# A gated mix of one-token attention and a dense layer: where w2's first half is loaded and multiplied

## The chip, the cores and the metric

The kernel runs on one core of a Trainium2 chip. The metric is the device time of one execution in microseconds (us), the median of several runs. Besides the times there is one profiled execution with its trace: TensorE's products (PE) and weight loads (PEld), VectorE (DVE), ScalarE (ACT), GpSimd (POOL), SyncE (SP, which issues nearly all loads), and the DMA engines. "Span" is the time from the first to the last instruction of that execution.

## The reference

One token with D = 576 values. The attention half has 32 query heads over 16 key/value heads, a window of the last 4096 keys and a head size of 128; the other half is a dense layer with 4608 hidden values and a GELU. A sigmoid gate mixes the two.

```python
g = sigmoid((x * gate_w).sum(-1, keepdims=True))
# A: attention on the last W = 4096 keys
q = x @ wq                                    # 32 heads of 128
k, v = k_cache[:, :, Sk - W:], v_cache[:, :, Sk - W:]
p = softmax(einsum("bhqd,bhkd->bhqk", q, k) * Dh ** -0.5)
a = einsum("bhqk,bhkd->bhqd", p, v).reshape(1, 1, 4096) @ wo
# B: the dense layer
b = gelu(x @ w1 + b1) @ w2 + b2
out = g * a + (1 - g) * b                     # [1, 1, 576]
```

All inputs are bfloat16. Everything is read once: w1 and w2 (5184 KB each), wq and wo (4608 KB each), and 16 MB each of keys and values, 53.6 MB in all.

## The kernel before

**Stages.** The kernel multiplies x by w1, builds the GELU's result `gt` (already scaled by 1 - g, 36 columns of 128 values), multiplies x by wq, and then goes through the keys in four groups of four key/value heads (`k_t`, 4096 KB each). VectorE transposes each half of a group (L550), TensorE makes the scores, ACT the exponentials. The values come in four tiles as well (`v_t`, 4096 KB each); `value_products(g)` (L660) multiplies tile g by the transposed probabilities, 32 products of 512 columns, in four column groups of the array side by side. `own_sums(g)` reduces the result on VectorE and `outputs(g)` (L694) brings it into `o_ps`. With all four, VectorE scales by the gate and the sums of the exponentials (`om`, `om_t`), five small products rearrange the heads into `ov_ps`, and two copies make `ov` (VectorE) and `ov_tail` (ACT).

**The end.** The result row is accumulated in `y_ps`. `y_add(vec, row)` (L384) adds one column of 128 values times one row tile of a weight: two products, 272 and 304 columns, in two column groups of the array, which run side by side. wo takes 4 such rows from a small part loaded apart (`wo_tail`, multiplied by `ov_tail`) and 31 from `wo_t` (multiplied by `ov`); w2 takes 36 (multiplied by `gt`), 18 in each half. Two copies and one store of 1.1 KB end the program.

**Order of the loads.** SyncE issues the loads in program order, each as soon as its buffer is free, and one queue serves them. The large buffers are four, tagged A to D. The keys take C, D, B, A, then values 0 and 1 take C and D (free when the keys in them are transposed), w2 takes B, values 2 A, values 3 C again (after value products 0), wo D (after value products 1). So the order behind the keys is: v0, v1, w2's first half (L646), v2, the two small loads of wo, v3, wo (L752), and w2's second half in four pieces of 10, 5, 2 and 1 rows (L757). A DMA tells of its landing by a semaphore; a small set of them is used in turn, so that an issue can also wait for an earlier load that has the same one.

**Order on TensorE.** The order is written out: `queue("pe", ...)` (L526) places each step behind the one queued before it. Around the change it is: value products 3; rows 0 to 5 of w2; outputs(3); rows 6 and 7; the five small products of `ov_ps`; rows 8 to 17; then the list `late` (L807): the four rows of `wo_tail`, one unused product, the 31 rows of `wo_t`, the 18 rows of w2's second half.

**The unused product.** `None` in `late` stands for a product of 512 f32 columns (the memory of the probabilities `p_t`, read as f32) by `ones`, written to `spare`, half of a PSUM tile that nobody reads (L815).

## Time and profile before

| what | value |
|---|---|
| median of 3 runs | 131.41 us (131.40 to 131.53) |
| the profiled execution | 131.67 us, its span 130.3 us |
| mean granted TensorE clock | 0.817 of full speed |
| DMA | 53.67 MB, mean 412 GB/s over the span |
| busy: PE, DVE, ACT, POOL | 79.3, 61.0, 11.5, 10.0 us |
| products of w2 rows (72) and wo_t rows (62) | 6.3 and 4.2 us busy |
| v2, v3 from issue to landing | 21.9 and 23.7 us |

Busy time of PE counts overlapping products once, and ends of products are modelled. The name of w1 and of w2 is shortened to `w_t` in the profile (digits are left out), `p_t` and `pt` are the probabilities, `s_ps` is any of the large PSUM tiles, and the tail of wo appears as `zeros`, the tile it lies in. A DMA's time "to landing" runs from its issue to its last semaphore update, and holds the time for which it waits behind earlier loads in the queue.

### The profile page before, as it was taken

How to read it: one execution, taken by the hardware profiler on the slowest of the kernel's cores; microseconds unless marked ns; L12 is line 12 of the kernel's file. 1: busy time of each engine (PE TensorE's matmuls, PEld its weight loads, DVE VectorE, ACT ScalarE, POOL GpSimd, SP SyncE). 2: the span in 40 equal slices, each digit the busy share in tenths (PEclk: the TensorE clock that was granted, in tenths of full speed). 3: DMA queues.
4: the chain of work that ended last, by engine and by line, in shares of the span. 5: the costliest groups of instructions: out<-in, count | busy, mean ns of one | idle time of the engine just before them, and what ended most of it. 6: DMA issues, size and time to landing. Idle time of an engine off the chain costs nothing.

```text
span 130.3 us, 1142 instructions
## 1 busy us (share of the span) xinstructions
PE 79.3 (61%) x538; PEld 26.2 (20%) x412; DVE 61.0 (47%) x50; ACT 11.5 (9%) x27; POOL 10.0 (8%) x32
## 2 busy tenths in 40 slices
PE   0003899297106996859949946995300840789794
PEld 0003012110100221211211210132200320245572
DVE  0030006215199769999999995145900050051001
ACT  3032100300300000030003003003000000000001
POOL 7009800100000000000000000000010000000000
PEclk9999999658755799985999995599655577579999
DMA  7999999899899999989989989999989999898970
GB/s 249 404 437 432 475 419 475 364 473 473 362 453 473 408 402 473 433 382 473 443 372 473 453 362 473 391 458 443 443 372 477 444 392 475 384 493 356 407 294 15
DMA packets 2503, 53.67 MB, mean 412 GB/s; under 512 B 286, under 2 KB 418, under 8 KB 708
## 3 DMA queue, kind: packets, MB, share of 16 engines
q1 hardware_dynamic: 2490, 53.61, 96.3%
q8 instruction: 3, 0.05, 0.2%
q10 hardware_dynamic: 10, 0.01, 0.0%
HBM read 53.62 MB, written 0.00 MB: 412 GB/s over the span
## 4 chain that ended last, share of the span: by engine, by line
DMA 60%; DVE 21%; PE 13%; issue 5%; ACT 0%; DVEq 0%
DMA k_t<-in_A_k_cache_dram 31%; DMA wo_t<-in_A_wo_dram 25%; DVE kt L550 15%; PE y_ps L386 5%; PE s_ps L572 5%; DMA rows<-in_A_x_dram 5%; DVE m L588 3%; DVE pt L621 2%; PE s_ps L662 1%; PE acc L662 1%; DVE mr L591 1%; ACT out_row L828 0%; PE mt_ps L597 0%; DVE negm L605 0%; DVEq L550 0%
## 5 line engine op out<-in xcount | busy, mean ns | idle before, releaser
L572 PE MATMUL s_ps<-kt,qz_flat 128*128 128x512 bf16 x128 | 35.3, 436 | 15.1 <-DVE kt L550 8.3
L550 DVE STREAM_TRANSPOSE kt<-k_t 128x4096 f32<-128x4096 f32 x8 | 35.3, 4432 | 4.8 <-DMA k_t<-in_A_k_cache_dram 4.8
L662 PE MATMUL s_ps<-v_t,pt 128*32 128x512 bf16 x96 | 9.1, 547 | 12.0 <-DMA v_t<-in_A_v_cache_dram 12.0
L572 PEld LDWEIGHTS <-qz_flat 128*128 128x128 bf16 x64 | 7.2, 112 | 40.6 <-issue 40.4
L676 DVE TENSOR_TENSOR own<-s_ps,is 128x512 f32<-128x512 f32 x3 | 2.1, 688 | 18.9 <-PE s_ps L662 18.9
L609 ACT ACTIVATE p_t<-s_ps,negm 128x1024 bf16<-128x1024 f32 x4 | 4.5, 1114 | 50.0 <-DVE negm L605 50.0
L662 PEld LDWEIGHTS <-pt 128*32 128x32 bf16 x128 | 3.7, 117 | 17.5 <-DMA v_t<-in_A_v_cache_dram 12.2
L342 PE MATMUL xs_ps<-ident,rows 1*128 1x1 bf16 x9 | 0.6, 189 | 10.8 <-POOL ident masks.py:199 10.8
L407 PE MATMUL s_ps<-w_t,x 128*32 128x512 bf16 x36 | 6.0, 611 | 1.6 <-DVE x L350 1.6
L588 DVE TENSOR_REDUCE m<-s_ps 128x1 f32<-128x1024 f32 x4 | 4.8, 1195 | 3.9 <-PE s_ps L572 3.9
L386 PE MATMUL y_ps<-w_t,gt 128*1 128x272 bf16 (+1 forms) x72 | 6.3, 304 | 0.0
L407 PE MATMUL s_ps<-wq_t,x 128*32 128x512 bf16 x36 | 4.9, 619 | 2.2 <-DMA wq_t<-in_A_wq_dram 2.2
L621 DVE STREAM_TRANSPOSE pt<-p_t 128x1024 bf16<-128x1024 bf16 x4 | 4.9, 1224 | 2.7 <-ACT p_t L609 2.7
L432 DVE STREAM_TRANSPOSE turned<-s_ps 128x1024 f32<-128x1024 f32 x2 | 2.5, 1249 | 7.3 <-PE s_ps L407 7.2
L829 DVE CAST out_row<-y_ps 1x272 bf16<-1x272 f32 x1 | 0.4, 429 | 10.2 <-PE y_ps L386 10.2
L713 POOL TENSOR_TENSOR ls<-is,sums 128x32 f32<-128x32 f32 x1 | 0.2, 240 | 63.9 <-ACT p_t L609 63.9
L697 PE MATMUL mt_ps<-is,summed 128*128 128x8 f32 x8 | 2.0, 319 | 4.6 <-DVE summed L686 4.6
L386 PE MATMUL y_ps<-wo_t,ov 128*1 128x272 bf16 (+1 forms) x62 | 4.2, 286 | 0.8 <-DMA wo_t<-in_A_wo_dram 0.8
L356 DVE CUSTOM_DVE_ANT_0 rows<-rows 1x576 bf16<-1x576 bf16 x1 | 0.7, 746 | 8.3 <-DMA rows<-in_gate_w_dram 8.3
L386 PEld LDWEIGHTS <-gt 128*1 128x1 bf16 x72 | 4.0, 89 | 1.9 <-issue 0.7
L686 DVE TENSOR_REDUCE summed<-own 128x128 f32<-128x512 f32 x4 | 4.2, 1044 | 0.1
L487 DVE STREAM_TRANSPOSE q_turned<-s_ps 128x1024 f32<-128x1024 f32 x2 | 2.4, 1228 | 3.8 <-PE s_ps L407 3.8
(83 smaller groups left out, 51.9 us busy)
## 6 DMA issues: line engine op xcount, KB each, us to landing
k_t<-in_A_k_cache_dram SPq DMA_DIRECT2D x4, 4096.0 KB, 33.9
v_t<-in_A_v_cache_dram SPq DMA_DIRECT2D x4, 4096.0 KB, 22.8
wq_t<-in_A_wq_dram SPq DMA_DIRECT2D x1, 4608.0 KB, 25.0
wo_t<-in_A_wo_dram SPq DMA_DIRECT2D x1, 4464.0 KB
w_t<-in_B_w_dram SPq DMA_DIRECT2D x1, 2880.0 KB, 14.4
w_t<-in_B_w_dram SPq DMA_DIRECT2D x1, 2592.0 KB, 23.6
w_t<-in_B_w_dram SPq DMA_DIRECT2D x1, 2304.0 KB, 8.3
w_t<-in_B_w_dram SPq DMA_DIRECT2D x1, 1440.0 KB
```

The costliest lines, as they stand in the source:

```text
L386: last = nc.tensor.matmul(y_out[s], lhsT=vec, rhs=row[:, DH:D] if s else row[:, 0:DH], start=start, stop=stop, skip_group_check=True,)
L407: nc.tensor.matmul(last[n][32 * g : 32 * g + 32], lhsT=vec, rhs=part(n), start=start and g0 == 0, stop=g0 + 4 + g >= len(pieces), skip_gro ...
L432: nc.vector.transpose(out=turned[:, c0 : c0 + n], in_=src[:].rearrange("p (q l j) -> p q j l", q=q, l=32),)
L487: nc.vector.transpose(out=q_turned[:, 1024 * c : 1024 * c + 1024], in_=q_s[c][:].rearrange("p (h l b) -> p h b l", l=32, b=2),)
L550: lambda: nc.vector.transpose(out=kt[g, f][:].bitcast(FP32), in_=keys.rearrange("p c d -> p (c d)").bitcast(FP32),),
L572: last = nc.tensor.matmul(s_ps[g][:, u * 512 : (u + 1) * 512].rearrange("p (c k) -> p c k", k=32), lhsT=qz(g, j, 2 * f + half), rhs=kv[:, ...
L588: queue("dve", lambda: nc.vector.reduce_max(out=m1[:], in_=s_ps[g][:], axis=AX.X))
L609: nc.scalar.activation(out=p_t[:].rearrange("p c k -> p (c k)"), in_=s_ps[g][:], func=ACT.Exp, bias=negm[:, 0:1], scale=SCALE, accum_out=s ...
L621: lambda: nc.vector.transpose(out=pt[:, g, :, :].rearrange("p c q -> p (c q)"), in_=p_t[:].rearrange("p c k -> p (c k)"),),
L662: last = nc.tensor.matmul(acc[g][32 * (c % 4) : 32 * (c % 4) + 32, :], lhsT=pt[:, g, c, :], rhs=v_t[g][:, c:NCK:32, :], start=(c < 4), sto ...
L676: lambda: nc.vector.tensor_tensor(out=own[:], in0=acc[g].rearrange("p (c d) -> p c d", c=4), in1=same_c.rearrange("p (c o) -> p c o", o=1) ...
L686: lambda: nc.vector.tensor_reduce(out=summed[g][:], in_=own[:].rearrange("p c d -> p d c"), axis=AX.X, op=ALU.add,),
```

## The change

The load of w2's first half moves from between v1 and v2 to behind wo. Its 18 rows, until now in three places among the value tile's steps, move into `late`, behind the 31 rows of `wo_t`. The one unused product between `wo_tail`'s rows and `wo_t`'s becomes four; one more of 512 columns goes behind `wo_t`'s rows, and one of 256 columns between the two halves of w2.

```diff
     v_t = [load("v_t", "CD"[g], A_v_cache, g) for g in range(2)]
-    nc.sync.dma_start(out=w2_t[:, 0:NJ, :], in_=w2_src[:, 0])
     v_t.append(load("v_t", "A", A_v_cache, 2))
...
+    nc.sync.dma_start(out=w2_t[:, 0:NJ, :], in_=w2_src[:, 0])
     for j0, j1 in ((0, 10), (10, 15), (15, 17), (17, 18)):
         nc.sync.dma_start(out=w2_t[:, NJ + j0 : NJ + j1, :], in_=w2_src[:, 1, j0:j1, :])
 
-    def w2_rows(f0, f1):
-        for f in range(f0, f1):
-            queue("pe", lambda: y_add(gt[:, f : f + 1], w2_t[:, f, :]))
-
-    w2_rows(0, 6)
     outputs(3)
...
-    w2_rows(6, 8)
     ov_ps = ps_m.tile([P, RO + 4], FP32, name="ov_ps", tag="m")
...
-    w2_rows(8, NJ)
     late = [(ov_tail, j, wo_tail[:, j, :]) for j in range(4)]
-    late.append(None)
+    late += [512] * 4
     late += [(ov, r, wo_t[:, r, :]) for r in range(RO)]
+    late += [512]
+    late += [(gt, f, w2_t[:, f, :]) for f in range(NJ)]
+    late += [256]
     late += [(gt, f, w2_t[:, f, :]) for f in range(NJ, NF)]
     for n, item in enumerate(late):
-        if item is None:
+        if isinstance(item, int):
             queue(
                 "pe",
                 lambda: nc.tensor.matmul(
-                    spare,
+                    spare[:, 0:item],
                     lhsT=ones[:],
-                    rhs=p_t[:].rearrange("p c k -> p (c k)").bitcast(FP32),
+                    rhs=p_t[:].rearrange("p c k -> p (c k)").bitcast(FP32)[:, 0:item],
                     start=True,
                     stop=True,
                 ),
```

## The prediction

> **What bounds the kernel now.** I read the profiled execution as a whole first, then its end. It took 131.67 us: a span of 130.3 us and 1.37 us around it. The median of the three timed runs is 131.41 us, so 0.26 us is taken off at the end of the sum. The page's 40 slices, in tenths:

> ```profile
> PEclk9999999658755799985999995599655577579999
> DMA  7999999899899999989989989999989999898970
> ```

> The DMA engines are full until the last few slices (53.67 MB at a mean of 412 GB/s), and TensorE's clock is at half speed for long stretches. The chain of waits (start us, us, what) ends so:

> ```profile
> 89.91 32.07 DMA wo_t<-in_A_wo_dram
> 121.97 0.04 issue
> 122.01 6.60 PE y_ps L386 x90
> 128.61 0.02 issue
> 128.63 0.40 ACT out_row L828
> ```

> As if TensorE's last 6.60 us set the end. The DMA view (KB each, us from issue to landing) and the view of the w2 and w1 loads (ns min/median/max, first and last start in us) correct that:

> ```profile
> w_t<-in_B_w_dram SPq DMA_DIRECT2D x1, 2592.0 KB, 23.6
> w_t<-in_B_w_dram SPq DMA_DIRECT2D x1, 288.0 KB, 36.2
> w_t<-in_B_w_dram SPq DMA_DIRECT2D x1, 144.0 KB, 27.0
> L757 SPq DMA_DIRECT2D w_t<-in_B_w_dram x4: 328/388/583, 90.5 to 101.3; - x4
> ```

> The last piece of w2 (144 KB, issued at 101.3) lands at 101.3 + 27.0 = 128.3, and in the same view the products with w2 start from 114.8 to 128.3. The end is a tie: the load queue drains just as TensorE reaches the last row. From there 0.3 us of products, 0.40 us of copy and the store follow in any version. So earlier work on TensorE gains nothing, and later work costs in full.

> TensorE's timeline between the last value tile and the end (start us, us, engine, line, tiles, count, idle before):

> ```profile
> 111.46 3.60 PE L662 MATMUL s_ps<-v_t,pt 128*32 128x512 bf16 x32 [4.29 <-DMA v_t<-in_A_v_cache_dram]
> 114.84 1.46 PE L386 MATMUL y_ps<-w_t,gt 128*1 128x272 bf16 x12
> 116.94 0.39 PE L697 MATMUL mt_ps<-is,summed 128*128 128x8 f32 x2 [0.63 <-DVE summed L686]
> 118.10 1.46 PE L386 MATMUL y_ps<-w_t,gt 128*1 128x272 bf16 x20
> 119.48 0.68 PE L386 MATMUL y_ps<-zeros,ov_tail 48*1 48x272 bf16 x8
> 120.09 1.12 PE L815 MATMUL s_ps<-p_t,ones 128*128 128x512 f32 x2
> 122.01 3.78 PE L386 MATMUL y_ps<-wo_t,ov 128*1 128x272 bf16 x59 [0.80 <-DMA wo_t<-in_A_wo_dram]
> ```

> The rows of w2's first half fill the gaps between 114.84 and 119.5. Twelve such products take 1.46 us at 114.84, twenty take 1.46 us at 118.10: the clock doubled in between. Half-microsecond windows (window, us, busy per engine, then granted clock, DMA share, GB/s) show when it changes:

> ```profile
> 85.00:85.50 0.50, 0.50 (x4) 0.04 (x1) 0.00 (x0) 0.00 (x0) 0.00 (x0) 0.82 0.68 290
> 105.50:106.00 0.50, 0.00 (x0) 0.00 (x0) 0.47 (x2) 0.00 (x0) 0.00 (x0) 0.84 0.46 197
> 109.00:109.50 0.50, 0.00 (x0) 0.00 (x0) 0.00 (x0) 0.00 (x0) 0.00 (x0) 0.57 0.78 334
> 115.50:116.00 0.50, 0.50 (x9) 0.43 (x4) 0.47 (x2) 0.00 (x0) 0.00 (x0) 0.60 0.99 429
> ```

> **The change, part by part.**

> *The moved load.* w2's first half is issued at 68.11 and lands 23.6 us later, at 91.7. Behind it v2 lands at 101.3, v3 at 111.4 and wo at 122.0 (the chain's row). v3 to wo is 4464 KB in 10.55 us, v2 to v3 4240 KB (v3 and the two small wo loads) in 10.1 us: 420 KB/us, so 2592 KB are 6.2 us. Without it ahead of them v2 lands at 95.1, v3 at 105.3, wo at 115.8; w2's first half takes wo's old place at 122.0, and the pieces behind it keep theirs, up to 128.3. The same bytes go through the same queue, so the last landing is unchanged: 0. The issue itself (0.33 us of SyncE) moves to about 90.5, ahead of the four pieces, which need not start before 122. SyncE's own waits show 9.2 us before the fourth piece until v2 lands; with one load fewer ahead in the turn of semaphores it is the third piece that waits for v2 (95.1), and the fourth for a small wo load: both before 102, and harmless. Cover in the queue: v2, issued at 79.37, had w2's half in front of it until 91.7, 12.3 us; now only v1 until 85.5, 6.1 us. The program's first load (2304 KB) took 8.3 us to land, of which 5.5 are transfer at 420 KB/us, so starting costs at most 2.8 us: 3.3 us are to spare, price 0. v3 (87.74) has v2 until 95.1, more than enough.

> *The removed rows.* 36 products leave the stretch 114.84 to 119.5 (1.46 + 0.42 + 1.46 us with the four at 117.26). TensorE stood idle 0.80 us at the end of it, waiting for wo: their place was free, so removing them frees nothing on the path. Added behind wo they do cost. wo's rows, from 122.01 to the last start at 125.89, are 30 steps of 0.129 us, so 18 rows (36 products, two side by side) are 2.3 us.

> *The unused products.* One of 512 columns holds TensorE from 120.09 to 121.15, its own weight loads included: 1.06 us at full clock. Four in a row are at most 4.2 us; at least 3.4 us, if their weight loads are hidden (a 512-column round of the value products at full clock is (1.91 - 0.38) / 7 = 0.22 us, and an f32 product of this row is two matmuls, each lasting one round longer, 592 against 379 ns, so four rounds each). I take 3.6, since the second weight load already runs under the first product. One of 256: half of 0.85 plus 0.2 of changeover, 0.6.

> *The sum.* Value tile 3 starts at 105.3. From its start (111.46) to ov_tail's copy (118.43 + 0.16) is 7.13 us, a chain through VectorE that the removed rows did not hold up: tail rows start at 112.4. At full clock: tail rows 0.6 (119.48 to 120.09), four products 3.6, wo's 31 rows 4.0, one product 1.06, w2's first 18 rows 2.3, the half product 0.6, the last 18 rows 2.3, end of the last product 0.2: 14.7 us, to 127.1. wo (115.8) and w2's first half (122.0) are there by the time they are wanted (116.6 and 121.7), or nearly. The landing bound is 128.3 + 0.3 = 128.6, as before. At full clock the change would be hidden, by 1.5 us.

> It will not be at full clock. Before, dense work from 111.46 on had raised it by 115.90, and nothing later let it fall. Now value tile 3 ends at 108.8 and TensorE has some 1 us of work until 112.4: a stretch like that of 105.66 to 109.07, after which the clock fell. The tail rows start at half speed, and stay there for T us, which costs T/2. T is 3.0 at break-even. Shortest: about 2.4, if a step falls just as they start (a stretch with 2.4 us of work, 78.35 to 81.77, did not raise it, one with about 2.6 of value products, 102.25 to 105.66, did). Longest: the 5.8 seen. The three seen give 2.2, 2.2 and 2.9 us of loss, 0.7 to 1.4 us beyond the cover; the short end gives none. I take T = 4.1, between the two ends: 127.1 + 2.05 = 129.15 against 128.60, **0.55 us later**. 131.67 + 0.55 - 0.26 = **131.95 us**. With T = 5.8 it is 132.8; with the products' upper price 0.6 more.

> [...]

> **Rivals.** *Hidden after all*: T at or below 3.4, or a shorter sum, and the queue sets the end: 131.4 us. For it: 1.5 us of cover, and a step at 109.07, as in this trace, lets the clock fall right at 112.5 and rise at 115.90, T = 3.5, a loss of 0.25 only. Against: two of the three rows. Chance 0.34. *Faster*: the queue ends unevenly; the DMA share falls to 0.60 at 125.5 and about 0.43 in the microsecond after 126, so if the new order evened out the engines the last landing could come up to 1.5 us sooner. TensorE allows 127.1 + 1.2 = 128.3, a gain of 0.3: 131.1 us, only where T is below 3. Against: each engine moves the same bytes in either order. 0.04. *The f32 products or one-column rows don't count as busy*: then half speed lasts through all four (8.4 us) and a stretch more, T about 11, 135.4 us. Against: the clock held at full speed from 115.90 to the end on little else. 0.03. *The queue runs dry* at v2, because starting costs more than 6.1 us in a full queue: each microsecond costs one, 132.4 us for one. 0.03.

> **How the numbers follow.** The forecast, late by 0.2 to 1.4 us, has 0.56. About 0.2% (0.26 us) is what a measurement of this kernel can tell from no change. Slower: 0.56 + 0.03 + 0.03 = 0.62; same: 0.34; faster: 0.04. The range reaches from just under the hidden case, 131.3, to the longest T, 132.9; the forecast's own is 131.6 to 132.9.

> **What would show it.** The last piece of w2 lands at 128.3 in both traces; value tile 3 starts at 105.3; wo's rows start at 117.5 to 119 with no wait for wo; the clock is 0.5 when the tail rows start and rises 2.4 to 5.8 us later; the last rows run without waiting for w2 and end 0.2 to 1.4 us after 128.6. I am wrong if TensorE waits for w2's last piece (hidden), if that piece lands elsewhere than at 128.3, or if the clock is already full at 112.4.

## The result, and the profile after

The changed kernel takes 132.77 us (median of 6 runs, 132.19 to 132.96) where the old one takes 131.41 (131.17 to 131.56): a ratio of 1.0096, 95% interval 1.0075 to 1.0118, or 1.36 us later. The profiled execution took 132.96 us with a span of 131.4. On another chip, beside the experiments below, it was 132.61 against 131.56 us. Medians here and below are of all runs, while ratios leave out a run that is more than 1.5% above the fastest of its kernel, as two runs of experiment 6 and two of experiment 9 are.

The end of the chain of waits of the changed kernel (start us, us, what):

```profile
86.67 18.08 DMA v_t<-in_A_v_cache_dram
104.75 0.04 issue
104.79 3.46 PE s_ps L661 x32
...
111.58 0.16 ACT ov_tail L798
111.75 0.04 issue
111.79 1.17 PE y_ps L386 x8
112.97 6.22 PE s_ps L811 x8
119.19 4.10 PE y_ps L386 x59
123.28 1.06 PE s_ps L811 x2
124.34 2.42 PE y_ps L386 x35
126.76 0.63 PE s_ps L811 x2
127.39 2.43 PE y_ps L386 x35
129.84 0.40 ACT out_row L824
```

No DMA stands between v3's landing and the end: from 111.79 on TensorE never waits. The old chain ended with a load of wo and products that just kept up with the last pieces of w2; this one ends with TensorE alone, at 129.84 in place of 128.61, 1.23 us later. Four unused products (L811 x8) take 6.22 us, and the rows of wo, which landed at 115.3, wait for them until 119.1. The copy of `ov_tail` is followed by eight tail products in 1.17 us, where they took 0.68 before.

Windows of the changed kernel (window, us, busy per engine, granted clock, DMA share, GB/s), cut at the clock's steps, which lie whole multiples of 3.41 us apart here as before (rises at 97.67, 107.91 and 118.15, falls at 101.08 and 111.32):

```profile
107.91:111.32 3.41, 1.15 (x15) 0.50 (x4) 2.14 (x4) 0.00 (x0) 0.00 (x0) 1.00 1.07 461
111.32:114.73 3.41, 2.94 (x10) 1.26 (x11) 0.19 (x1) 0.16 (x1) 0.00 (x0) 0.50 0.93 401
114.73:118.15 3.42, 3.42 (x5) 1.35 (x4) 0.00 (x0) 0.00 (x0) 0.00 (x0) 0.50 1.00 423
```

Full speed until 111.32, since the step ahead of it (104.49 to 107.91) held 3.12 us of value tile 3; then half speed for two whole steps, to 118.15. The first of these had TensorE busy for 2.94 of 3.41 us and still did not raise the clock. The tail rows started at 111.79, so half speed lasted T = 118.15 - 111.79 = 6.36 us of the 18 that follow.

The loads moved as worked out: v2 in use at 95.07, v3 at 104.79, wo landed at 115.3. The 288 KB piece, issued at 95.05, landed 32.4 us later, at 127.4; the last piece followed at 127.8, where the old order had 127.9 and 128.3.

### The profile page after: what moved, and what is told of

It is laid out like the page before. It is cut to its first block, busy times and chain, and to the rows that moved or that the text cites. A ratio compares the mean times of both kernels' runs of the same rounds, so it can differ in the third digit from the quotient of the medians.

```text
span 131.4 us, 1161 instructions
## 1 busy us (share of the span) xinstructions
PE 81.8 (62%) x548; PEld 28.8 (22%) x422; DVE 61.0 (46%) x50; ACT 11.5 (9%) x27; POOL 10.0 (8%) x32
## 4 chain that ended last, share of the span: by engine, by line
DMA 49%; PE 22%; DVE 22%; issue 5%; ACT 0%; DVEq 0%
DMA k_t<-in_A_k_cache_dram 31%; DVE kt L550 15%; DMA v_t<-in_A_v_cache_dram 14%; PE y_ps L386 8%; PE s_ps L811 6%; PE s_ps L572 4%; DMA rows<-in_A_x_dram 4%; PE s_ps L661 3%; DVE m L588 3%; DVE pt L621 2%; PE acc L661 1%; DVE summed L685 1%; DVE mr L591 1%; DVE own L675 1%; ACT out_row L824 0%
## 5 line engine op out<-in xcount | busy, mean ns | idle before, releaser
L572 PE MATMUL s_ps<-kt,qz_flat 128*128 128x512 bf16 x128 | 32.1, 407 | 17.9 <-DVE kt L550 9.7
L661 PE MATMUL s_ps<-v_t,pt 128*32 128x512 bf16 x96 | 8.5, 519 | 6.8 <-DMA v_t<-in_A_v_cache_dram 6.8
L811 PE MATMUL s_ps<-p_t,ones 128*128 128x512 f32 (+1 forms) x12 | 8.1, 817 | 0.0
L386 PE MATMUL y_ps<-w_t,gt 128*1 128x272 bf16 (+1 forms) x72 | 5.0, 286 | 0.0
L386 PEld LDWEIGHTS <-gt 128*1 128x1 bf16 x72 | 3.9, 83 | 1.5 <-issue 1.1
L386 PE MATMUL y_ps<-wo_t,ov 128*1 128x272 bf16 (+1 forms) x62 | 4.2, 286 | 0.0
## 6 DMA issues: line engine op xcount, KB each, us to landing
w_t<-in_B_w_dram SPq DMA_DIRECT2D x1, 2592.0 KB
```

Of the source, the lines that this page charges most:

```text
L386: last = nc.tensor.matmul(y_out[s], lhsT=vec, rhs=row[:, DH:D] if s else row[:, 0:DH], start=start, stop=stop, skip_group_check=True,)
L572: last = nc.tensor.matmul(s_ps[g][:, u * 512 : (u + 1) * 512].rearrange("p (c k) -> p c k", k=32), lhsT=qz(g, j, 2 * f + half), rhs=kv[:, ...
L661: last = nc.tensor.matmul(acc[g][32 * (c % 4) : 32 * (c % 4) + 32, :], lhsT=pt[:, g, c, :], rhs=v_t[g][:, c:NCK:32, :], start=(c < 4), sto ...
L811: lambda: nc.tensor.matmul(spare[:, 0:item], lhsT=ones[:], rhs=p_t[:].rearrange("p c k -> p (c k)").bitcast(FP32)[:, 0:item], start=True, ...
```

## Experiments

All are edits of the changed kernel unless it is said. None leaves out or changes a part of the result. Times are medians; each ratio is against the kernel before, run beside it on the same chip.

**1. Without any unused product.**

```diff
-    late += [512] * 4
     late += [(ov, r, wo_t[:, r, :]) for r in range(RO)]
-    late += [512]
     late += [(gt, f, w2_t[:, f, :]) for f in range(NJ)]
-    late += [256]
```

> The changed kernel without any of its unused products; nothing of the result is left out. Theory (unused products at half clock push TensorE's last rows behind the last landing): wo's rows start when wo lands, at 115.3 us of the trace, at half speed, and 8.8 us of rows plus at most 3.4 us for the slow clock end by 127.5, before the last landing at 127.8: 131.0 to 131.4 us. Rival 1 (one-column rows don't count as busy, so that without f32 products the clock never rises): 115.3 + 17.6 = 132.9 in place of 129.8, some 135.8 us. Rival 2 (the later load of w2's first half costs the time by itself): 132.8 us as for the changed kernel.

Measured: 131.34 us (131.18 to 131.47), ratio 0.9992 (0.9983 to 1.0002). TensorE's timeline (start us, us, engine, line, tiles, count, idle before):

```profile
112.13 0.68 PE L386 MATMUL y_ps<-zeros,ov_tail 48*1 48x272 bf16 x8 [0.47 <-ACT ov_tail L798]
115.50 6.14 PE L386 MATMUL y_ps<-wo_t,ov 128*1 128x272 bf16 x62 [2.69 <-DMA wo_t<-in_A_wo_dram]
121.66 2.49 PE L386 MATMUL y_ps<-w_t,gt 128*1 128x272 bf16 x36
125.13 1.46 PE L386 MATMUL y_ps<-w_t,gt 128*1 128x272 bf16 x20 [0.98 <-DMA w_t<-in_B_w_dram]
126.88 1.39 PE L386 MATMUL y_ps<-w_t,gt 128*1 128x272 bf16 x16 [0.29 <-DMA w_t<-in_B_w_dram]
```

wo's rows run at half speed for two thirds of their time (6.14 us in place of 4.2), and still TensorE waits for w2 twice. The whole loss is gone, so the later load costs nothing by itself (rival 2 falls). The clock rose at 119.55 after a step filled with one-column rows alone (116.14 to 119.55: busy 3.41 us at a clock of 0.50, and 1.00 from there; rival 1 falls).

**2. The four ahead of wo, without the later one and a half.**

```diff
     late += [(ov, r, wo_t[:, r, :]) for r in range(RO)]
-    late += [512]
     late += [(gt, f, w2_t[:, f, :]) for f in range(NJ)]
-    late += [256]
```

> The changed kernel with the four unused products ahead of wo, without the one behind wo and the half one in w2. Theory: 1.06 + 0.63 us less behind 119.1, so the rows end at 128.15, where the last landing would let them end too (127.8 + 0.3): 131.1 to 131.4 us. Rival (the move of the load costs the time): 132.8 us.

131.46 us (131.23 to 131.60, and one run of ten at 132.79), ratio 1.0008 (0.9985 to 1.0031): hidden. In this trace the four products took 5.38 us, wo's rows started at 118.18, and TensorE waited 0.58 and 0.29 us for w2 at the end.

**3. One ahead of wo in place of four.**

```diff
-    late += [512] * 4
+    late += [512]
```

> The changed kernel with one unused product ahead of wo in place of four; the one behind wo and the half one stay. Theory: wo's rows start at 115.3, at half speed until the clock rises, and the rest ends at about 127.3, before the last landing: 131.0 to 131.4 us. Rival 1 (the clock rises only for f32 products): wo's rows take 8 us, and all ends at about 131 or later: 134 us or more. Rival 2 (the load's move): 132.8 us.

131.50 us (131.29 to 132.28), ratio 1.0024 (1.0004 to 1.0043). The theory holds for the median run, slightly above its range; three of ten runs are at 132.1 to 132.3 us, which it had not foreseen. In two of these three the span (129.9 and 130.1 us) is as short as in the other runs, so what lengthened them lies outside the span; the third has a span of 130.7. No trace shows any of them. Rivals 1 and 2 fall.

**4. The products alone**, in the kernel before, with load and rows in their old places (the loop that reads `late` takes numbers as in the changed kernel and is left out here).

```diff
-    late.append(None)
+    late += [512] * 4
     late += [(ov, r, wo_t[:, r, :]) for r in range(RO)]
+    late += [512, 256]
...
```

> The kernel before, load and rows in their old places, with the changed kernel's unused products: four ahead of wo's rows, one and a half behind them. Theory (products ahead of wo's rows have only the wait for wo as room): at full clock 3.6 us from 120.1, then 4.0 of wo, 1.7 of products and 2.5 of w2 rows: end at 131.9 in place of 128.6, 134.7 us. Rival (the load's move makes the loss, the products are hidden): 131.4 us.

134.54 us, ratio 1.0236 (1.0223 to 1.0249). The end of its chain, up to TensorE's last row:

```profile
119.76 3.63 PE s_ps L816 x8
123.39 4.10 PE y_ps L386 x59
127.49 1.49 PE s_ps L816 x4
128.98 2.43 PE y_ps L386 x35
```

The load is where it was, and the loss is 3.1 us: the unused products pay in full wherever TensorE has no slack. It also prices them at full clock: 3.63 us for four, against 6.22 in the changed kernel.

**5. Filling the gaps to keep the clock up.** A product of 448 columns behind value tile 3, and one of 64 and one of 128 in the two other gaps; `fill(n)` queues one product of n columns of `p_t` by `ones`, written to `spare`.

```diff
+    fill(448)
     outputs(3)
...
+    fill(64)
     ov_ps = ps_m.tile([P, RO + 4], FP32, name="ov_ps", tag="m")
...
+    fill(128)
     late = [(ov_tail, j, wo_tail[:, j, :]) for j in range(4)]
```

> The changed kernel with three further unused products (448, 64 and 128 columns) where w2's rows had been, so that TensorE is busy from value tile 3 to the tail rows. Theory: the clock is at full speed when the tail rows start (112.0), all products and rows take 14.3 us, to 126.3, so that the last landing sets the end: 131.0 to 131.4 us, in spite of more products. Rival (the products' number, not the clock, makes the loss): 132.8 us or more.

133.00 us, ratio 1.0138 (1.0094 to 1.0182). This says nothing against the theory, because the experiment did not do what it was meant to:

```profile
109.33 1.86 PE L762 MATMUL s_ps<-p_t,ones 128*128 128x448 f32 x2 [0.80 <-DVE own L675]
110.98 0.43 PE L696 MATMUL mt_ps<-is,summed 128*128 128x8 f32 x2
```

`spare` lies in the PSUM tile of value tile 3, so the product waited until VectorE had read that tile, and then held outputs(3) back to 110.98 (110.09 in the changed kernel). The four products behind the tail rows took 5.07 us, against 3.70 at full clock (the timeline of experiment 4): by that the clock rose at about 116.7, an estimate.

**6. The same without the wait.** One product of 448 columns, into the half tile of value tile 2, whose reader is long done.

```diff
+    queue(
+        "pe",
+        lambda: nc.tensor.matmul(
+            acc12[:, 512:960],
+            lhsT=ones[:],
+            rhs=p_t[:].rearrange("p c k -> p (c k)").bitcast(FP32)[:, 0:448],
+            start=True,
+            stop=True,
+        ),
+    )
     outputs(3)
```

> The changed kernel with one further unused product of 448 columns right behind value tile 3, into a PSUM half whose reader is long done, so that it waits for nothing and ends (110.1) before outputs(3) can start. Theory (half clock under the unused products makes the loss): value tile and product are 5.1 us of unbroken work, any step of 3.41 us in it finds the threshold of some 2.5 us, the tail rows start at full clock at 112, wo's rows at 116.3, and the last landing sets the end: 131.2 to 131.5 us, with more unused products than the changed kernel. Rival (their number makes it, whatever the clock): 132.8 us or more.

132.87 us, ratio 1.0078 (1.0049 to 1.0107), but the runs lie from 131.33 to 133.65. The profiled one is among the shortest, with a span of 130.0 us (windows as above):

```profile
107.31:110.73 3.42, 3.34 (x16) 0.94 (x8) 1.74 (x2) 0.00 (x0) 0.00 (x0) 0.50 0.99 428
110.73:114.14 3.41, 2.56 (x18) 1.31 (x16) 0.60 (x3) 0.16 (x1) 0.00 (x0) 1.00 0.96 413
```

Where the step falls right, the clock is full at the tail rows (0.68 us for the eight), four products take 3.70 us and nothing is lost, with more unused work than the changed kernel has. That is against the rival. Nine of the twelve runs took 132.6 us or more, which is against my expectation of "any step". No trace shows one of them. Two reasons can be given, neither of them shown. The room is scant: with 2.55 us taken as what raises the clock, my estimate from the steps listed in the last section, 5.1 us of work hold that much within one step of 3.41 for steps ending anywhere in 5.1 + 3.41 - 2 x 2.55 = 3.41 us, which leaves no margin for the small gaps between the products. And a rise can come too soon: in the changed kernel the clock rose at 107.91, after 3.12 us of value tile 3, and had fallen again at 111.32, just ahead of the tail rows.

**7. The tail rows from 128 partitions**, the added ones zero in both operands.

```diff
-    ov_tail = const.tile([48, 4], BF16, name="ov_tail")
-    nc.scalar.copy(out=ov_tail[:], in_=ov_ps[0:48, RO : RO + 4])
+    ov_tail = const.tile([P, 4], BF16, name="ov_tail")
+    nc.gpsimd.memset(ov_tail[:].bitcast(FP32), 0.0)
+    nc.scalar.copy(out=ov_tail[0:48, :], in_=ov_ps[0:48, RO : RO + 4])
...
-    late = [(ov_tail, j, wo_tail[:, j, :]) for j in range(4)]
+    tail_all = zeros[:, NZ : NZ + 4 * D].rearrange("p (j n) -> p j n", j=4)
+    late = [(ov_tail, j, tail_all[:, j, :]) for j in range(4)]
```

> The changed kernel with the tail rows multiplied from 128 partitions in place of 48 (the others hold zeros in both operands; the result is the same). Theory A (rows of 48 partitions hardly count as busy, which is why the stretch 111.32 to 114.73 with 2.65 us of work did not raise the clock): now they count in full, T is 1.1 us shorter on the mean, 0.5 us less, 132.2 us. Theory B (f32 products count less than others): no change, 132.8 us.

132.50 us (131.61 to 132.94), ratio 1.0090 (1.0072 to 1.0107): between what A and B give, and the interval overlaps those of the changed kernel, so the time decides nothing. The trace, of the shortest of the six runs, has a matching pair. Here (windows as above):

```profile
111.61:115.02 3.41, 2.94 (x12) 1.27 (x11) 0.19 (x1) 0.16 (x1) 0.00 (x0) 0.50 1.03 443
115.10:117.00 1.90, 1.90 (x6) 0.92 (x5) 0.00 (x0) 0.00 (x0) 0.00 (x0) 1.00 0.99 412
```

The same 2.94 us busy as in the step 111.32 to 114.73 of the changed kernel, in the same phase of the program, and this time the clock rises. The difference is the tail rows' partitions: theory A, as far as one pair goes. Counted in columns as in the last section, the two steps held 2.65 and 2.60 us, close to where steps were seen to go either way, so the pair alone would be weak; that section has stronger evidence from products of 2 partitions.

**8. The four ahead of the tail rows.**

```diff
-    late = [(ov_tail, j, wo_tail[:, j, :]) for j in range(4)]
-    late += [512] * 4
+    late = [512] * 4
+    late += [(ov_tail, j, wo_tail[:, j, :]) for j in range(4)]
```

> The changed kernel with the four unused products ahead of the tail rows. They wait for no copy, so they start at 111.4. Theory A (48-partition rows hardly count): the count starts 1.5 us earlier, T between 2.5 and 5.9 us from 111.4, the rows end at 127.4 to 129.1 against a landing bound of 128.15: 131.3 to 132.3 us, median about 131.6. Theory B (f32 products count less): the rise comes at 3.0 us or later, and only the 0.4 us of earlier start are gained: 132.3 us or more.

132.10 us (131.33 to 132.67), ratio 1.0042 (1.0020 to 1.0064): about half the loss, in A's range but above its median, and below B's. TensorE in the profiled execution, the shortest of the twelve:

```profile
111.49 5.38 PE L811 MATMUL s_ps<-p_t,ones 128*128 128x512 f32 x8
116.80 0.68 PE L386 MATMUL y_ps<-zeros,ov_tail 48*1 48x272 bf16 x8
```

The products took 5.38 us against 3.70 at full clock (the timeline of experiment 4), so that by estimate half speed lasted 3.4 us of them, and the tail rows ran at full speed behind them (0.68 us).

**9. Filling the long gap ahead of value tile 3 as well.** Two products of 512 columns behind outputs(2), one of 448 behind value tile 3, all into the half tile of experiment 6 (here `fill(n)` writes there).

```diff
     outputs(2)
+    fill(512)
+    fill(512)
     queue("pe", lambda: value_products(3))
     own_sums(3)
+    fill(448)
```

> The changed kernel with three further unused products: two of 512 columns between outputs(2) and value tile 3, where TensorE stood idle, and one of 448 behind value tile 3. Theory (half clock under the unused products makes the loss): unbroken work from 101 to 108 holds two whole steps of 3.41 us, enough for every place of the grid, so that the clock is full before the tail rows in every run, and the last landing sets the end: 131.2 to 131.5 us, without the scatter of the changed kernel. Rival (the number of unused products makes it): 132.8 us or more, as they are now eight.

131.71 us beside 131.56 of the kernel before, ratio 1.0006 (0.9997 to 1.0016): in nine of eleven runs (131.35 to 131.84) the loss is gone, with some eight unused products in place of five and a half. For these the rival falls. The other two took 133.33 and 133.70 us, longer than any run of the changed kernel; no trace shows them, and "every run" was too much to say. Nor does the profiled run go as I had said (windows as above):

```profile
105.54:108.95 3.41, 3.41 (x33) 1.23 (x26) 0.29 (x1) 0.00 (x0) 0.00 (x0) 0.50 0.90 387
108.95:112.37 3.42, 1.83 (x13) 0.72 (x11) 2.05 (x5) 0.16 (x1) 0.00 (x0) 1.00 1.14 491
112.37:115.78 3.41, 3.41 (x11) 1.39 (x8) 0.00 (x0) 0.00 (x0) 0.00 (x0) 0.50 0.89 383
```

The work was not unbroken: TensorE still waited 1.35 us for v3 ahead of 105.00. The clock is full from 108.95, but the gaps behind value tile 3 (0.74, 0.37 and 0.47 us without a product) let it fall again at 112.37, when the tail rows have just begun (112.19). What the filling secures is the next step: it is 3.41 us long, full of work, and ends the half speed at 115.78, so T is 3.6. A loss of 1.8 us is about what the wait for the last landing covers.

**10. The changed kernel once more**, beside 9.

> The changed kernel itself, beside the others on one chip. Theory: the steps of the clock lie differently in each run, so the times scatter over about 131.6 to 133.2 us with a median of 132.7. Rival (one place of the steps for all runs): times within 0.3 us of each other.

132.61 us (131.97 to 133.06), ratio 1.0065 (1.0042 to 1.0087): a scatter of 1.1 us, where the kernel before has 0.5 on this chip. The rival falls. The profiled execution is the longest of the six, and its steps lie differently:

```profile
105.34 3.60 PE L661 MATMUL s_ps<-v_t,pt 128*32 128x512 bf16 x32 [4.00 <-DMA v_t<-in_A_v_cache_dram]
112.75 1.17 PE L386 MATMUL y_ps<-zeros,ov_tail 48*1 48x272 bf16 x8 [0.47 <-ACT ov_tail L798]
```

Here the clock did not rise during value tile 3 at all. The four products took 5.51 us against 3.70 at full clock (the timeline of experiment 4): by that it rose at about 117.5, so T was about 4.7 us and not 6.36. Yet the rows ended at 129.98 (129.84 at T = 6.36), because the tail rows started 0.96 us later: v3 was in use 0.55 us later, and the small products behind it ran at half speed (0.60 us for the pair at 110.83, where the changed kernel's first trace has 0.39).

**11. Experiment 1 with the small loads of wo over more DMA engines.**

```diff
-    for h0, h1, at, k in ((0, 16, 0, 4), (16, Hq, 32, 4)):
+    for h0, h1, at, k in ((0, 16, 0, 8), (16, Hq, 32, 8)):
```

> The changed kernel without unused products, with the two small loads of wo split over 8 DMA engines each in place of 4. Theory: in all traces seven of the sixteen engines finish the last pieces about 1.3 us behind the other nine; spread wider, the small loads delay the late ones by half, the last landing comes up to 0.4 us sooner, and since TensorE only waits for it here, the time falls with it: 131.0 us. Rival (the late engines are late for another reason): 131.3 us.

132.51 us (131.97 to 133.69), ratio 1.0088 (1.0051 to 1.0126). A miss, the other way: the last landing came at 128.6 in place of 127.9. The trace does not show that the wider split did it: v2, issued ahead of the small loads, was already in use 0.7 us later than in experiment 1 (95.78 against 95.08). As in experiment 1, TensorE waits for w2 twice at the end (0.54 and 0.29 us), so the loss of the profiled run is the queue's, not that of unused products; the other seven runs have no trace. What makes engines late at the end stays open.

## Why the prediction was right, and where its size was not

Right: the old end was a tie of queue and TensorE, and the new order turned it into TensorE alone. Right: the moved load costs nothing and the queue does not run dry (experiment 1). Right: the gaps that w2's rows had filled let the clock fall (1.00 until 111.32, 0.50 from there to 118.15), and the four unused products ran at half speed (6.22 us, 3.63 in experiment 4). Two ways of removing that loss, taking products out (all of them in 1, the later one and a half in 2) and cutting the half speed short with more of them (9, nine of eleven runs), removed the whole 1.0%.

The step that was mis-sized is "I take T = 4.1". T was 6.36 us in the profiled execution, beyond "the 5.8 seen" that I had as its longest. That is 1.1 us of TensorE's end. The sum itself holds: 111.79 + 14.7 + 6.36 / 2 = 129.67, and 129.84 was measured. In the second trace of the changed kernel (10) T was about 4.7 and the sum holds as well: 112.75 + 14.7 + 4.7 / 2 = 129.80, and 129.98 was measured.

A second term was off the other way: the tail rows started at 111.8 in place of 112.4, mostly because v3 was in use at 104.79 and not at 105.3. That the measured time lies within the range is owed in part to this: with the tail rows at 112.4, T = 6.36 would have given 127.1 + 3.18 = 130.28, and 133.1 us, above the range. The landing bound was 128.1 (127.8 + 0.3) in place of 128.6, because the old order's 128.3 had been carried over. By my own sign the forecast was wrong there, since the last piece landed elsewhere than at 128.3; it made no difference, because TensorE ended later. Both traces of the changed kernel and those of 1, 6 and 9 have the last piece between 127.8 and 128.3.

Why T was longer: I counted the tail rows as work that raises the clock. They hardly do (the pair of 7, and the last section), so the count began only with the unused products, 1.1 us later and at half speed. From there a step must still hold some 2.5 us of them, an estimate from the steps of the last section (it rose after 2.45, 2.48 and 2.59 us of such work). T is then at least 1.1 + 2.5 = 3.6 and at most 1.1 + 2.5 + 3.41 = 7.0, unless the clock was still up for the tail rows themselves; the middle, 5.3, would have given 1.15 us of loss in place of 0.55.

Where the steps lie was not the same in any two of five traces: counted from the start of the span the clock rose at 115.90 in the trace before, at 118.15, 119.55, 110.73 and 115.02 in those of the changed kernel and experiments 1, 6 and 7, which are different places on a grid of 3.41. The scatter of the times fits that: the changed kernel's runs lie over 1.1 us (experiment 10), those of experiment 1, where the end waits for the landing, over 0.3.

*Hidden* (0.34) did not happen, though 2, 3 and 9 show how near it was: 1.7 us of products fewer, and it would have. *Faster* did not either: the last landing did come 0.45 us sooner in the profiled execution, but TensorE was 2 us behind it, and experiment 1, which waits for the landing, gains 0.08% with an interval that includes none. The products' count as work was settled the other way round from the third rival: f32 products raise the clock (the step from 114.73 to 118.15 held nothing else), 48-partition rows hardly. Whether an f32 product counts as fully as a bf16 one of the same time is not shown.

No version here beats the kernel before; experiment 1 equals it with less work.

## What to carry to other kernels

Where the end is a tie between a full load queue and an engine, an order that moves the same bytes and does not bring the last landing forward has little to gain, and what fills an engine's wait must be priced at the clock it will really get. Filler products are no cover for the clock if they stand on the chain: put them where the engine idles anyway, as experiment 9 did, long enough to fill a whole step (3.41 us here), into memory that no reader still holds. Even there two of eleven runs were long. The wait that they replace should be measured against their half-speed price, here 6.2 us and not 3.6.

## What the runs showed of the hardware

In the trace of the changed kernel the clock changed at 90.84, 97.67, 101.08, 107.91, 111.32 and 118.15, whole multiples of 3.41 us apart, as it did in the trace before (the prediction's 85.18, 105.66, 109.07 and 115.90). How much work each step of 3.41 us held is my estimate: each product's time is taken as its columns, 0.213 us for 512 at full speed (592 less 379 ns, as in the prediction) and twice that at a clock of 0.50, f32 counted twice a matmul, side by side counted once. Among steps with products of 128 partitions alone it rose after 2.45 us (experiment 1, 105.90 to 109.31: the small products behind took 0.39 us, where those at half speed took 0.59), 2.48 (before, 102.25 to 105.66) and 2.59 (changed, 94.25 to 97.67), and not after 2.37 (before, 78.35 to 81.77) or 2.51 (experiment 7, 94.54 to 97.96: the small products behind took 0.60 us). No single value parts these five, and "nearly all of the stretch" in the prediction was too much for the first three. It fell after 1.20 us (changed, 87.43 to 90.84) and held after 1.30 (changed, 63.53 to 66.95).

In these traces products of few partitions counted less. The rows of 48 in experiment 7 are a hint; the early products of 2 partitions (`s_ps<-rows,ident 2*32`) show it more clearly. In the changed kernel (windows as above):

```profile
19.16:22.57 3.41, 2.70 (x9) 0.81 (x9) 2.74 (x3) 0.00 (x0) 0.00 (x0) 1.00 1.20 519
22.57:25.99 3.42, 1.10 (x8) 0.76 (x8) 0.47 (x2) 1.41 (x7) 0.48 (x2) 0.50 0.78 335
63.53:66.95 3.42, 1.59 (x9) 0.59 (x5) 3.38 (x3) 0.00 (x0) 0.00 (x0) 1.00 1.05 450
66.95:70.36 3.41, 2.15 (x10) 0.48 (x5) 3.41 (x3) 1.20 (x2) 0.00 (x0) 1.00 1.07 461
```

The first step held 1.53 us by columns, 0.75 of it in products of 2 partitions, and the clock fell all the same, where 1.30 us of products of 128 partitions in the third step held it. In the trace before, the clock fell at 23.74 after a step of 1.42 us, 0.64 of it in products of 2 partitions. That few columns of the array are in use is not the reason: in experiment 1 the step from 116.14 to 119.55 held one-column rows of 128 partitions alone, and the clock rose. The windows count modelled ends of products, so that the first step looks busy for 2.70 us and yet lost the clock.
